# A DFT and MLP kernel: four of eight blocks of the first DFT as seven products, means added by transfers, the MLP begun by token halves

## The chip, the cores and the metric

The kernel runs on one core of one Trainium2 chip. The metric is the time on the device in microseconds. PE is TensorE, DVE VectorE, ACT ScalarE, POOL GpSimd; SP issues most transfers.

## The reference

All is float32: 2048 tokens (S) of 512 features (D), an MLP of 1792 hidden units (F).

```python
xn = layernorm(x)
a = einsum("bsd,ed->bse", xn, dft_hid_re)      # first DFT, along the features
b = einsum("bsd,ed->bse", xn, dft_hid_im)
s = einsum("ts,bse->bte", dft_seq_re, a) - einsum("ts,bse->bte", dft_seq_im, b)
h = gelu(einsum("bsd,df->bsf", layernorm(xn), w1) + b1)
g = silu(einsum("bsf,fd->bsd", h, w2) + b2)
out = x + s * g
```

## The kernel before

Each float32 operand is split into a rounded part `hi` (ACT, L64) and the rest `lo` (DVE, L65), and each product is three matmuls: hi hi, hi lo, lo hi. Big tiles are 128 x 2 x 512 floats from one pool of 39 (`operand`, `guest`); PSUM has eight banks of 128 x 512 in the first stage. The order on each engine is that of the code, written out by hand; engines and queues work in order.

**First DFT.** Row block i is 128 tokens, blocks of four row blocks are "blocks" b of 512 tokens. For each of 16 row blocks and each of the two matrices (m) `dft_mm` (L305) adds 12 matmuls into one bank: four blocks of features, three terms each. `dft_out` (L328) copies the bank out on ACT with the row's factor and leaves the store in a list that is four long (LAG) before SP issues it. Row blocks 0 to 3 are centred and transposed on PE (`first_x`, `first_transpose`); for blocks 1 to 3 the transposed input `xT` is loaded (`xt_load`), and DVE subtracts the row of means (`xt_centre`, L265), after which `xt_make` splits it. A row of means comes from statistics on DVE (L106), is turned on PE (`rows_turn`, L169), copied by ACT, written to DRAM (L173) and read back by SP with a broadcast over the partitions (`row_load`, L177). The factors are computed in small DVE operations (`rstd`). The row R holds the factors of the second layernorm.

**Operands of the MLP.** In the second half of that stage DVE scales the centred `xT` by R (`y_scale`, L409) and makes the sums t1 to t4 of its quarters (`y_sum`, L421); `y_split` splits 11, t1, t2, 21, 22, t3, t4. The first MLP layer then needs seven block products for eight, in chunks j of 7: `h_product` (L518), each 24 matmuls over two halves of tokens (tau). `w1_sums` and `w1_split` make w1's operands of a chunk. After each product `h_after` copies or adds a PSUM tile. The second layer (L684) and the DFT along the sequence (L684, L1002), both by seven products, follow.

Products are numbered as in the code: 1, 6, 7 and 4 accumulate on one PSUM tile ("y"), 5 and 3 on "z", 2 on "x"; the partial sums are taken out between them.

Of the kernel before, what the change touches and what calls it, by code (L numbers as in the profile page):

```python
# [15 lines left out]
P = 128  # L16
# [6 lines left out]
def fnet_mixer_kernel(ctx: ExitStack, tc: tile.TileContext, x, xT, ct, wt, w1, w2, b1, b2, out):  # L23
# [71 lines left out]
    r1 = consts.tile([P, NS], F32, name="r1")  # L95
    nr1 = consts.tile([P, NS], F32, name="nr1")
    r2 = consts.tile([P, NS], F32, name="r2")
    v2 = consts.tile([P, NS], F32, name="v2")
# [11 lines left out]
    def rstd(r, var, i, n):  # L110
        v = small.tile([P, n], F32, tag="v", name="v")
# [3 lines left out]
        ops = [  # L115
            lambda: nc.vector.tensor_scalar(v, var, EPS, None, op0=ALU.add),
            lambda: nc.vector.tensor_scalar(h.bitcast(I32), v.bitcast(I32), 1, None, op0=ALU.logical_shift_right),
            lambda: nc.vector.tensor_scalar(y.bitcast(I32), h.bitcast(I32), -1.0, float(RSQRT_MAGIC), op0=ALU.mult,
                                            op1=ALU.add),
            lambda: nc.vector.tensor_scalar(h, v, -0.5, None, op0=ALU.mult),  # L120
        ]
        for k in range(4):
            dst = r[:, i:i + n] if k == 3 else y
            ops += [
                lambda: nc.vector.tensor_mul(t, y, y),
                lambda: nc.vector.tensor_mul(t, t, h),
                lambda dst=dst: nc.vector.scalar_tensor_tensor(dst, t, 1.5, y, op0=ALU.add, op1=ALU.mult),
            ]
        return ops


    def weave(chain, others):
        n = max(len(chain), len(others))
        at = 0
        for q, o in enumerate(chain):
            o()
            while at * len(chain) < (q + 1) * len(others):
                others[at]()
                at += 1
        for o in others[at:]:  # L140
            o()

    def r1_chain(i, n):
        return rstd(r1, mv1[:, i:i + n, 1], i, n) + [
            lambda: nc.vector.tensor_scalar(nr1[:, i:i + n], r1[:, i:i + n], -1.0, None, op0=ALU.mult)]

    def r2_chain():
        return [lambda: nc.vector.tensor_mul(v2, mv1[:, :, 1], r1),  # L150
                lambda: nc.vector.tensor_mul(v2, v2, r1)] + rstd(r2, v2, 0, NS) + [
                lambda: nc.vector.tensor_mul(r2, r2, r1)]
# [43 lines left out]


# [3 lines left out]
    def x_load(i):  # L201
        if i % 2 == 0:
            x_two[i // 2] = guest(f"x{i}")
        xs[i] = x_two[i // 2][:, i % 2, :]
        nc.sync.dma_start(out=xs[i], in_=x[i * P:(i + 1) * P, :])

    raw_w = []


    def load_w(m, k2):  # L210
        t = room(f"rw{m}{k2}")
        for k in (2 * k2, 2 * k2 + 1):
            (nc.scalar if m == 0 and k % 2 else nc.sync).dma_start(out=t[:, k % 2, :], in_=wt[m, k])
            raw_w.append(t[:, k % 2, :])

# [41 lines left out]
    def xt_load(b):  # L257
        for k2 in range(NK // 2):
            xtr[b, k2] = guest(f"xT{b}_{k2}")
            nc.sync.dma_start(out=xtr[b, k2], in_=xT[b, 2 * k2:2 * k2 + 2].rearrange("k p w -> p k w"))  # L260
# [25 lines left out]
    MEANS = {1: "m1", 2: "m02", 3: "m3"}  # L286

    def m_pack(b):
        rows_pack([mv1[:, block(int(c)), 0] for c in MEANS[b][1:]], MEANS[b])

    def m_turn(b):
        rows_turn(MEANS[b])
        blocks = [int(c) for c in MEANS[b][1:]]
        for c, row in zip(blocks, row_load(MEANS[b], len(blocks))):
            mrow[c] = row
# [27 lines left out]

    def dft_out(i, m):
# [3 lines left out]
        nc.scalar.activation(e, dacc.pop((i, m)), AF.Copy, scale=(nr1 if m else r1)[:, i:i + 1])  # L328
        stores.append(((b_d if m else a_d)[i // 2][i % 2], e))
# [23 lines left out]
    xt_load(1)  # L353

# [8 lines left out]
    m_pack(1)  # L363
    first_x(3)
    dft_mm(1, 1)
    m_turn(1)
    weave(r1_chain(0, 2 * NC), [])
# [5 lines left out]
    for q in range(2 * NC, 3 * NC):  # L373
        x_load(q)
# [3 lines left out]
    def xt_prepare(b, ks):  # L378
        for k in ks:
            xt_centre(b, k)  # L380
        for k in ks:
# [25 lines left out]
    def y_scale(k2, bs):  # L407
        for b in bs:
            nc.vector.tensor_mul(xtr[b, k2], xtr[b, k2], both(rrow[b]))  # L409
            y_raw[(("11", "12"), ("21", "22"))[k2][b // 2], b % 2] = xtr[b, k2]  # L410

    def y_split(name):
        y_op[name] = [split_two(y_raw[name, tau], f"y{name}_{tau}") for tau in range(2)]

    def y_sum(dst, a, b):
        for tau in range(2):
            if dst == "t1":
                y_raw["t1", tau] = guest(f"yt1_{tau}")
            if dst in ("t2", "t3", "t4"):
                y_raw[dst, tau] = y_raw[{"t2": "t1", "t3": "12", "t4": "t2"}[dst], tau]  # L420
            nc.vector.tensor_sub(y_raw[dst, tau], y_raw[a, tau], y_raw[b, tau])  # L421

    for i in range(3, NS):
        b, c = divmod(i, NC)
        chain, bulk = [], []
        if b == 0:
            xt_prepare(1, range(NK // 2))
        elif b + 1 < NB:
            if i == 4:
                xt_load(2)  # L430
            if i == 6:
                xt_prepare(2, (0, 1))
            if i in (8, 9):
                xt_prepare(3, (i - 8,))
        if i == 4:
            for q in range(3 * NC, 4 * NC):
                x_load(q)
            early.close()
            wr = early.enter_context(tc.tile_pool(name="wr", bufs=1, reuse_waits="tile"))
            wp = early.enter_context(tc.tile_pool(name="wp", bufs=4, reuse_waits="tile"))  # L440
            lp = early.enter_context(tc.tile_pool(name="lpm", bufs=2, reuse_waits="tile"))
            w1_load(0)
        if i in (4, 5):
            bb = i - 2
            bulk = [lambda q=q: stats(mv1, xs[q], q) for q in range(bb * NC, (bb + 1) * NC)
                    ] + [lambda: m_pack(bb)]
        if i == 6:
            xt_load(3)
        if i == 7:
            chain = r1_chain(2 * NC, 2 * NC) + r2_chain()  # L450
            xt_load(0)
        if i == 10:
            for k2 in range(2):
                xt_centre(0, k2)
        if i == 11:
            y_scale(0, (0, 1, 2))
        if i == 12:
            y_scale(0, (3,))
            y_split("11")
            y_sum("t1", "12", "11")  # L460
        if i == 13:
            y_split("t1")
            y_scale(1, (2, 3))
        if i == 14:
            y_sum("t2", "22", "t1")
            y_split("t2")
        if i == 15:
            y_sum("t3", "22", "12")
            y_scale(1, (0, 1))
        weave(chain, bulk)  # L470
        if i == 7:
# [586 lines left out]
```

## Time and profile before

| | |
|---|---|
| median of 3 runs | 675.45 us (675.4 to 675.48) |
| span of the profiled execution | 673.0 us |
| first matmul of the first DFT | 6.18 us |
| first matmul of the MLP | 96.39 us |
| transfers | 171.49 MB, mean 255 GB/s |

Each row of a timeline has the start and the duration in us, engine, line, operation, the tile written and those read, their shapes, how many in a row, and in brackets how long the engine stood idle before and what ended that. "PEld" is the load of a stationary operand. A row that ends in "q" after the engine is a transfer being issued. In a row of windows each pair is busy time and number of instructions for PE, PEld, DVE, ACT and POOL, then the granted clock of PE, the busy share of the transfer engines and GB/s. The clock stays at full speed in the stage in question.

### The profile page before, as it was taken

How to read it: one execution, taken by the hardware profiler on the slowest of the kernel's cores; microseconds unless marked ns; L12 is line 12 of the kernel's file. 1: busy time of each engine (PE TensorE's matmuls, PEld its weight loads, DVE VectorE, ACT ScalarE, POOL GpSimd, SP SyncE). 2: the span in 40 equal slices, each digit the busy share in tenths (PEclk: the TensorE clock that was granted, in tenths of full speed). 3: DMA queues.
4: the chain of work that ended last, by engine and by line, in shares of the span. 5: the costliest groups of instructions: out<-in, count | busy, mean ns of one | idle time of the engine just before them, and what ended most of it. 6: DMA issues, size and time to landing. Idle time of an engine off the chain costs nothing.

```text
span 673.0 us, 8182 instructions
## 1 busy us (share of the span) xinstructions
PE 665.8 (99%) x2933; PEld 547.5 (81%) x2933; DVE 538.3 (80%) x595; ACT 346.9 (52%) x366; POOL 47.0 (7%) x80
## 2 busy tenths in 40 slices
PE   8999999999999999999999999999999999999996
PEld 5888888888888888888888888888888888888885
DVE  7877887777778755887988998729978399998995
ACT  4443666445454665565546555446445454646540
POOL 1000000122112100000000100000000001210100
PEclk9999999999999999999999999999999999999999
DMA  8667731899998999588799997406545548996883
GB/s 312 225 222 233 261 131 58 311 331 327 329 337 305 415 376 362 188 281 289 277 371 409 390 321 255 157 32 196 190 154 146 127 123 259 303 257 243 307 259 126
DMA packets 69896, 171.49 MB, mean 255 GB/s; under 512 B 6592, under 2 KB 20960, under 8 KB 69856
## 3 DMA queue, kind: packets, MB, share of 16 engines
q1 hardware_dynamic: 58304, 132.67, 56.4%
q0 software_dynamic: 11200, 37.76, 17.2%
q8 instruction: 23, 0.38, 0.2%
q10 hardware_dynamic: 352, 0.54, 0.2%
q14 instruction: 17, 0.14, 0.1%
HBM read 120.60 MB, written 50.35 MB: 254 GB/s over the span
## 4 chain that ended last, share of the span: by engine, by line
PE 97%; DVE 1%; DMA 1%; issue 0%; ACT 0%; SPq 0%; DVEq 0%
PE pz L684 19%; PE px L684 18%; PE pd L305 12%; PE ma L684 11%; PE hy L518 11%; PE mb L684 8%; PE hz L518 6%; PE pw L684 5%; PE hx L518 3%; PE px L1002 2%; PE pw L1002 2%; DVE W L279 1%; DMA rw<-wt 1%; PE pt L250 0%; DVE zr L1007 0%
## 5 line engine op out<-in xcount | busy, mean ns | idle before, releaser
L790 DVE TENSOR_TENSOR c<-c,c 128x1024 f32<-128x1024 f32 x32 | 39.0, 1218 | 3.2 <-DMA c<-ct 3.2
L65 DVE TENSOR_TENSOR w1l<-w1r,w1h 128x1792 fp32r<-128x1792 f32 x7 | 14.2, 2025 | 24.5 <-ACT w1h L64 24.5
L65 DVE TENSOR_TENSOR R_b1l<-c,R_b1h 128x1024 fp32r<-128x1024 f32 x16 | 19.4, 1221 | 13.9 <-ACT R_b1h L64 10.6
L305 PE MATMUL pd<-W,xt_0h 128*128 128x512 f32 x96 | 29.8, 392 | 0.0
L684 PE MATMUL pw<-R_s1h,L 128*128 128x512 f32 x96 | 29.7, 389 | 0.0
L305 PE MATMUL pd<-W,xt_1h 128*128 128x512 f32 x96 | 29.6, 389 | 0.0
L64 ACT ACTIVATE R_s3h<-c 128x1024 fp32r<-128x1024 f32 x16 | 17.0, 1061 | 23.6 <-DVE c L790 9.5
L64 ACT ACTIVATE R_b2h<-c 128x1024 fp32r<-128x1024 f32 x16 | 16.9, 1059 | 21.5 <-DVE c L795 13.4
L523 ACT ACTIVATE hc<-hc,b_t 128x1024 f32<-128x1024 f32 x14 | 16.1, 1153 | 20.3 <-DVE hc L558 19.7
L65 DVE TENSOR_TENSOR R_s2l<-c,R_s2h 128x1024 fp32r<-128x1024 f32 x16 | 19.5, 1221 | 8.6 <-PE pz L684 8.6
L64 ACT ACTIVATE R_s2h<-c 128x1024 fp32r<-128x1024 f32 x16 | 17.0, 1061 | 16.7 <-PE px L684 9.3
L65 DVE TENSOR_TENSOR R_s3l<-c,R_s3h 128x1024 fp32r<-128x1024 f32 x16 | 19.5, 1219 | 3.9 <-PE pz L684 3.9
L64 ACT ACTIVATE R_s1h<-c 128x1024 fp32r<-128x1024 f32 x16 | 16.4, 1051 | 11.7 <-DVE c L801 11.7
L64 ACT ACTIVATE R_b1h<-c 128x1024 fp32r<-128x1024 f32 x16 | 16.6, 1052 | 11.0 <-PE pz L684 5.5
L64 ACT ACTIVATE R_a1h<-c 128x1024 fp32r<-128x1024 f32 x16 | 16.9, 1054 | 8.9 <-PE pz L684 7.2
L305 PEld LDWEIGHTS pd<-W,xt_1h 128*128 128x128 f32 x96 | 18.0, 188 | 3.8
L684 PEld LDWEIGHTS pw<-R_s1h,L 128*128 128x128 f32 x96 | 18.0, 188 | 3.7
L798 POOL DMA_DIRECT2D c<-ct x8 | 6.9, 868 | 201.5 <-issue 141.6
L305 PEld LDWEIGHTS pd<-W,xt_0h 128*128 128x128 f32 x96 | 17.8, 188 | 4.0
L65 DVE TENSOR_TENSOR R_b2l<-c,R_b2h 128x1024 fp32r<-128x1024 f32 x16 | 19.4, 1218 | 1.5 <-PE px L684 1.5
L65 DVE TENSOR_TENSOR R_a1l<-c,R_a1h 128x1024 fp32r<-128x1024 f32 x16 | 19.5, 1219 | 1.3 <-PE px L684 1.1
L65 DVE TENSOR_TENSOR R_s4l<-c,R_s4h 128x1024 fp32r<-128x1024 f32 x16 | 19.5, 1218 | 0.7 <-PE px L684 0.7
(886 smaller groups left out, 2172.9 us busy)
## 6 DMA issues: line engine op xcount, KB each, us to landing
c<-ct SPq DMA_DIRECT2D x68, 512.0 KB, 5.9
m<-h_d SPq DMA_DIRECT2D x48, 512.0 KB, 6.8
h_d<-ht POOLq DMA_DIRECT2D x21, 512.0 KB, 7.6
s_d<-sa SPq DMA_DIRECT2D x32, 256.0 KB, 4.0
la<-s_d SPq DMA_DIRECT2D x32, 256.0 KB, 5.5
h_d<-hc POOLq DMA_DIRECT2D x13, 512.0 KB, 4.0
x<-x SPq DMA_DIRECT2D x16, 256.0 KB, 5.0
xT<-xT SPq DMA_DIRECT2D x8, 512.0 KB, 6.1
```

What stands on the lines that cost most here:

```text
L64: nc.scalar.activation(hi, src, AF.Copy)
L65: nc.vector.tensor_sub(lo, src, hi.bitcast(F32))
L279: nc.vector.tensor_sub(lo, raw_w[n], hi.bitcast(F32))
L305: nc.tensor.matmul(acc, xt[i, k][px], weights[m * NK + k][pw], start=n == 0, stop=n == len(terms) - 1)
L518: nc.tensor.matmul(acc[:, tau, :], w[:, W1_AT[p], k * P:(k + 1) * P], r[:, k, :], start=p in (1, 5, 2) and i == 0, stop=p in (2, 3, 4) and ...
L523: nc.scalar.activation(dst, src, AF.Gelu_apprx_tanh, bias=b1_t[:, row:row + 1])
L684: nc.tensor.matmul(acc[k][:, tau, :], a, c[:, tau, :], start=first and i == 0, stop=last and i == len(terms) - 1, skip_group_check=True)
L790: nc.vector.tensor_sub(t, t, raw)
L798: nc.gpsimd.dma_start(out=t, in_=ct[1, 1, n], accum_op=ALU.add)
L1002: nc.tensor.matmul(acc[KEY[name]][k][:, tau, :], a[k], c[:, tau, :], start=False, stop=u == us[-1] and i == 2, skip_group_check=True)
```

## The change

Row blocks 0 to 7 (now the token blocks 0 and 2, by `tok`) go through `dft_mm` as before. The other eight (token blocks 1 and 3) are computed behind them as seven block products of 24 matmuls (`q_product`): left operands are the split MLP operands of token half 1 (`y_op[name, 1]`), right ones the split sums of the DFT matrices' quarters, which `a_sums` makes and `a_split` splits. As the MLP operands carry the second layernorm's factor, `q_after` multiplies by a factor `qq` that takes it off: for products 1, 5, 6, 4 a copy on ACT, for 2, 3, 7 a `scalar_tensor_tensor` on DVE that adds a bank to the copy. Product 4 accumulates on the bank that product 7's `q_after` has read.

Only block 1 is still centred by DVE and split as a DFT operand. For the other three the negative means are written over a tile with a broadcast (SP, two loads of 256 KB) and `xT` is added to it by an accumulating transfer on POOL's queue (`centred_load`). Row blocks 12 to 15 get their statistics from two activations with an accumulated sum on ACT (`act_stats`).

The DVE operations that make operands are handed to `q_product` as steps, one behind each block of four. The first chunk of the MLP runs all products but the fourth on token half 1 (ONE), then on half 0 (ZERO); w1 is loaded and split during the seven products, where before it was done in row blocks 4 to 10.

The core of the diff (in the loop, only what stands there now; the lines removed are printed above):

```diff
+    def second_factors():
+        for make, at in ((outer, 0), (inner, HB)):
+            make(vv[:, at:at + NC], mv1[:, HB:HB + NC, 1], 1.0)
+            make(vv[:, at + NC:at + HB], sq, 1.0 / D)
+        rsqrt(rr[:, 2 * HB:], vv, 2 * HB)
+    def last_factors():
+        nc.vector.tensor_mul(qq, vv[:, :HB], rr[:, 2 * HB:3 * HB])
+        nc.vector.tensor_mul(qq, qq, rr[:, 3 * HB:])
+        nc.vector.tensor_scalar(nq, qq, -1.0, None, op0=ALU.mult)
...
+    TB = (0, 2, 1, 3)
+    def tok(i):
+        return TB[i // NC] * NC + i % NC
...
+    NEG = {2: 0, 3: 1, 0: 2}
+    def neg_means(b):
+        nc.vector.tensor_scalar(nm[:, block(NEG[b])], mv1[:, block(b), 0], -1.0, None, op0=ALU.mult)
+    def act_stats(i):
+        t = guest(f"as{i}")
+        c = i % NC
+        nc.scalar.activation(t[:, 0, :], xs[i], AF.Copy, scale=-1.0 / D, accum_out=nm[:, NC + c:NC + c + 1])
+        nc.scalar.activation(t[:, 1, :], xs[i], AF.Square, bias=nm[:, NC + c:NC + c + 1], accum_out=sq[:, c:c + 1])
+    def centred_load(b):
+        row = row_d["n"][0, NEG[b] * W:(NEG[b] + 1) * W].partition_broadcast(P)
+        for k2 in range(NK // 2):
+            t = xtr[b, k2] = guest(f"xT{b}_{k2}")
+            for k in range(2):
+                nc.sync.dma_start(out=t[:, k, :], in_=row)
+            nc.gpsimd.dma_start(out=t, in_=xT[TB[b], 2 * k2:2 * k2 + 2].rearrange("k p w -> p k w"), accum_op=ALU.add)
...
     xt_load(1)
+    for q in range(NC):
+        x_load(3 * NC + q)
...
-    m_turn(1)
-    weave(r1_chain(0, 2 * NC), [])
+    m_turn()
+    first_factors()
...
-    for q in range(2 * NC, 3 * NC):
-        x_load(q)
+    act_stats(3 * NC)
+    act_stats(3 * NC + 1)
+    for q in range(NC):
+        x_load(2 * NC + q)
...
+    def y_scale(k2, b):
+        nc.vector.tensor_mul(xtr[b, k2], xtr[b, k2], both(rrow[b]))
+        y_raw[f"{k2 + 1}{b % 2 + 1}", b // 2] = xtr[b, k2]
+    def y_split(name, tau):
+        y_op[name, tau] = split_two(y_raw[name, tau], f"y{name}_{tau}")
+    def y_sum(dst, tau):
+        place, a, b = {"t1": ("11", "12", "11"), "t2": ("t1", "22", "t1"), "t3": ("12", "22", "12"),
+                       "t4": ("t2", "21", "t2")}[dst]
+        t = y_raw[dst, tau] = y_raw[place, tau]
+        nc.vector.tensor_sub(t, y_raw[a, tau], y_raw[b, tau])
+    a_op = {}
+    def a_sums():
+        a11, a12, a21, a22 = (room_w[m, k2] for m in range(2) for k2 in range(2))
+        nc.vector.tensor_add(a22, a21, a22)
+        nc.vector.tensor_sub(a21, a11, a21)
+        nc.vector.tensor_sub(a11, a22, a11)
+        nc.vector.tensor_sub(a12, a12, a11)
+    def a_split(p):
+        m, k2 = {5: (1, 1), 6: (0, 0), 3: (0, 1), 7: (1, 0)}[p]
+        hi, lo = split_two(room_w[m, k2], f"A{p}")
+        a_op[p] = [(hi[:, k, :], lo[:, k, :]) for k in range(2)]
+    RIGHT = {1: "11", 2: "21", 3: "22", 4: "t4", 5: "t1", 6: "t2", 7: "t3"}
+    qx, q_part = {}, {}
+    def q_place(name, c):
+        if c % 2 == 0:
+            q_part[name, c] = guest(f"q{name}_{c}")
+        return q_part[name, c - c % 2][:, c % 2, :]
+    def q_out(i, m, e):
+        stores.append((dft_at(i, m), e))
+        while len(stores) > LAG:
+            store()
+    def q_after(p, c):
+        i, j = 2 * NC + c, 3 * NC + c
+        f, g = (qq[:, t - HB:t - HB + 1] for t in (i, j))
+        nf, ng = (nq[:, t - HB:t - HB + 1] for t in (i, j))
+        acc = qx[{1: "y", 6: "y", 7: "y", 4: "y", 5: "z", 3: "z", 2: "x"}[p], c]
+        if p in (1, 5, 6, 4):
+            e = q_place(p, c)
+            nc.scalar.activation(e, acc, AF.Copy, scale={1: f, 5: ng, 6: g, 4: nf}[p])
+            if p == 4:
+                q_out(i, 1, e)
+        else:
+            e = q_part[{2: 1, 3: 6, 7: 5}[p], c - c % 2][:, c % 2, :]
+            nc.vector.scalar_tensor_tensor(e, acc, {2: f, 3: g, 7: ng}[p], e, op0=ALU.mult, op1=ALU.add)
+            q_out(*{2: (i, 0), 3: (j, 0), 7: (j, 1)}[p], e)
+    def q_product(p, steps=()):
+        key = {1: "y", 6: "y", 7: "y", 4: "y", 5: "z", 3: "z", 2: "x"}[p]
+        yh, yl = y_op[RIGHT[p], 1]
+        for c in range(NC):
+            if p in (1, 5, 2):
+                qx[key, c] = bank(f"q{key}{c}")
+            cols = slice(c * P, (c + 1) * P)
+            terms = [(a[:, k, cols], w) for k in range(2)
+                     for a, w in ((yh, a_op[p][k][0]), (yh, a_op[p][k][1]), (yl, a_op[p][k][0]))]
+            for n, (a, w) in enumerate(terms):
+                nc.tensor.matmul(qx[key, c], a, w, start=p in (1, 5, 2) and n == 0,
+                                 stop=p in (2, 3, 4) and n == len(terms) - 1, skip_group_check=True)
+            q_after(p, c)
+            if c < len(steps):
+                steps[c]()
+    for i in range(3, HB):
+        if i == 3:
+            xt_prepare(1)
+            act_stats(3 * NC + 2)
+            act_stats(3 * NC + 3)
+            for q in range(NC):
+                stats(mv1, xs[2 * NC + q], 2 * NC + q)
+            neg_means(2)
+            neg_means(0)
         if i == 4:
+            second_factors()
+        if i == 5:
+            a_sums()
+            last_factors()
         if i == 6:
+            y_scale(0, 2)
+            y_split("11", 1)
         if i == 7:
+            y_scale(1, 2)
+            y_split("21", 1)
+            a_split(5)
         dft_mm(i, 0)
         dft_out(i - 1, 1)
+        if i == 5:
+            row_st["R"] = rr[:, HB:3 * HB]
             rows_turn("R")
+            rrow = [None] * 2 + row_load("R", 2, 2)
         dft_mm(i, 1)
         dft_out(i, 0)
+        if i == 4:
+            row_st["n"] = nm
+            rows_turn("n")
+            centred_load(2)
+            centred_load(3)
+    dft_out(HB - 1, 1)
+    for p, (m, k2) in {1: (0, 0), 2: (0, 1), 4: (1, 1)}.items():
+        a_op[p] = [weights[m * NK + 2 * k2 + k] for k in range(2)]
+    y_scale(0, 3)
+    y_sum("t1", 1)
+    y_split("t1", 1)
+    q_product(1, [lambda: y_scale(1, 3), lambda: y_sum("t2", 1)])
+    rrow[0:2] = row_load("R", 2)
+    centred_load(0)
+    q_product(2, [lambda: y_split("t2", 1), lambda: a_split(6)])
+    q_product(5, [lambda: y_split("22", 1), lambda: a_split(3), lambda: y_sum("t3", 1), lambda: y_split("t3", 1)])
+    q_product(6, [lambda: a_split(7), lambda: y_sum("t4", 1), lambda: y_split("t4", 1)])
+    early.close()
+    wr = early.enter_context(tc.tile_pool(name="wr", bufs=1, reuse_waits="tile"))
+    wp = early.enter_context(tc.tile_pool(name="wp", bufs=4, reuse_waits="tile"))
+    lp = early.enter_context(tc.tile_pool(name="lpm", bufs=2, reuse_waits="tile"))
+    w1_load(0)
+    q_product(3, [lambda: y_scale(0, 0), lambda: y_scale(0, 1), lambda: y_split("11", 0)])
+    def w1_make(j):
+        w1_sums(j)
+        w1_split(j)
+        w1_load(j + 1)
+    q_product(7, [lambda: y_sum("t1", 0), lambda: w1_make(0), lambda: y_split("t1", 0)])
+    q_product(4, [lambda: y_scale(1, 1), lambda: y_sum("t2", 0), lambda: y_split("t2", 0), lambda: y_scale(1, 0)])
...
+    ONE, ZERO = slice(1, 2), slice(0, 1)
+    h_seq = [(0, p, s) for s in (ONE, ZERO) for p in (1, 5, 6, 2, 3, 7)]
+    for j in range(1, NJ):
+        h_seq += [(j, 1, TAUS), (j, 5, TAUS), (j - 1, 4, TAUS), (j, 6, TAUS), (j, 2, TAUS), (j, 3, TAUS), (j, 7, TAUS)]
+    y_late = {(1, ONE): lambda: y_split("21", 0),
+              (5, ONE): lambda: y_split("22", 0),
+              (6, ONE): lambda: y_sum("t3", 0),
+              (2, ONE): lambda: y_split("t3", 0),
+              (3, ONE): lambda: w1_make(1),
+              (3, ZERO): lambda: (y_sum("t4", 0), y_split("t4", 0))}
```

`h_product` and `h_after` take the halves as a slice, with the same matmuls.

More of the change, by code (lines that the diff above doesn't have):

```diff
@@ L122, in rstd @@
-        for k in range(4):
[L123 to L141, printed above, removed]
@@ new lines, in outer, with first_factors @@
+    def outer(dst, var, scale):
+        nc.vector.tensor_scalar(dst, var, scale * (1.0 + EPS), EPS * EPS, op0=ALU.mult, op1=ALU.add)
+    def first_factors():
+        v = small.tile([P, 2 * HB], F32, tag="v", name="v")
+        inner(v[:, :HB], mv1[:, :HB, 1], 1.0)
+        outer(v[:, HB:], mv1[:, :HB, 1], 1.0)
+        rsqrt(rr[:, :2 * HB], v, 2 * HB)
+        nc.vector.tensor_scalar(nr1, rr[:, :HB], -1.0, None, op0=ALU.mult)
+    def second_factors():
[3 more added lines that the diff above has]
+        rsqrt(rr[:, 2 * HB:], vv, 2 * HB)
@@ L327, in dft_out @@
         e = e_two[i][:, m, :]
-        nc.scalar.activation(e, dacc.pop((i, m)), AF.Copy, scale=(nr1 if m else r1)[:, i:i + 1])
-        stores.append(((b_d if m else a_d)[i // 2][i % 2], e))
+        nc.scalar.activation(e, dacc.pop((i, m)), AF.Copy, scale=(nr1 if m else rr)[:, i:i + 1])
+        stores.append((dft_at(i, m), e))
         while len(stores) > LAG:
```

207 lines of the change are left out of this document (67 added, 140 removed).

## The prediction

> **What bounds the kernel now.** I read the busy times, the chain of waits, the waits of PE, then the timeline of the first 125 us, where the change lies, and the transfers last.
>
> ```profile
> span 673.0 us, 8182 instructions
> ...
> PE 665.8 (99%) x2933; PEld 547.5 (81%) x2933; DVE 538.3 (80%) x595; ACT 346.9 (52%) x366; POOL 47.0 (7%) x80
> ...
> PE 97%; DVE 1%; DMA 1%; issue 0%; ACT 0%; SPq 0%; DVEq 0%
> ...
> PE idle_ps L189 <- DVE warm L217: 1.2, 1, 1.2
> PE pd L320 <- ACT xt L64: 0.4, 1, 0.4
> PE pt L250 <- DVE xc L240: 0.3, 1, 0.3
> ...
> 96.39 0.39 PE L518 MATMUL hy<-y_0h,w1h 128*128 128x512 f32 x1
> ...
> 99.11 0.39 PE L518 MATMUL hz<-yt_0h,w1h 128*128 128x512 f32 x1
> ```
>
> PE is the bound, and it waits 1.9 us in all, before 7 us. So every matmul taken away is worth its full slot, and every new wait of PE costs its full length. Twelve matmuls lie between the two starts: 2.72 / 12 = 0.227 us each. The MLP starts at 96.39, right behind the first DFT: that is the mark against which I place the new stage.
>
> **What is removed.** Blocks of 24 matmuls: 16 row blocks before (384), now 8 (192) and 7 products of 4 x 6 (168). 24 fewer x 0.227 = -5.44 us. One transpose of rows fewer (m1, n, R for four) is about -0.25. If nothing else changed, the time would fall to 669.8.
>
> **New ACT work ahead of block 4.** The four `act_stats` activations of row blocks 12 and 13 stand on ACT between the copies of row block 1 and that of 2, so ahead of the rounding `xt_0h`, for which PE waits.
>
> ```profile
> 2.03 0.20 ACT L218 ACTIVATE warm<-warm 128x1 f32<-128x1 f32 x1
> ...
> 6.29 2.71 ACT L278 ACTIVATE W<-rw 128x512 fp32r<-128x512 f32 x5
> ...
> 25.93 0.72 ACT L328 ACTIVATE e<-pd,r 128x512 f32<-128x512 f32 x1
> ...
> 26.80 1.06 ACT L64 ACTIVATE xt_0h<-xT 128x1024 fp32r<-128x1024 f32 x1 [0.15 <-DVE xT L265]
> ...
> 29.04 1.22 DVE L65 TENSOR_TENSOR xt_1l<-xT,xt_1h 128x1024 fp32r<-128x1024 f32 x1
> ...
> 30.43 0.41 PEld L305 LDWEIGHTS pd<-W,xt_0h 128*128 128x128 f32 x2
> ...
> 31.79 0.41 PEld L305 LDWEIGHTS pd<-W,xt_1l 128*128 128x128 f32 x2
> ...
> 18.00:20.00 2.00, 2.00 (x11) 1.55 (x10) 1.86 (x6) 0.27 (x1) 0.00 (x0) 1.00 0.00 0
> ```
>
> No row shows an activation with an accumulated sum. From below: five 128x512 copies in 2.71, a pace of 0.52, so 2.1 for four. From above: the longest copy of that shape, 0.72, and a small operation of 0.20, so 3.7. I take the middle, 2.9. `xt_1l` ends at 30.26 and is loaded at 31.79, a margin of 1.53, and ACT has 0.15 of slack before `xt_0h`. `first_factors` is one small operation longer and twice as wide, 0.3. So PE waits 2.9 + 0.3 - 1.53 - 0.15 = 1.5 us (0.7 to 2.3) as row block 4 starts. The moved loads of x cost nothing: the transfers stand still from 18 to 20 us, which covers the extra 1 MB; without that cover the m1 row would be late by up to some 3 us.
>
> **The way of the means (n).** They are turned behind row block 4: 30.43 + 1.5 + 24 x 0.227 = 37.4.
>
> ```profile
> 38.81 0.27 PE L169 MATMUL rpm<-ident,rsm 128*8 128x128 f32 x1
> ...
> 40.64 0.32 SPq L177 DMA_DIRECT2D rowm<-rdm  x1
> ...
> rowR<-rdR SPq DMA_DIRECT2D x2, 512.0 KB, 5.3
> z_d<-z POOLq DMA_DIRECT2D x2, 512.0 KB, 3.3
> ...
> rowm<-rdm SPq DMA_DIRECT2D x2, 256.0 KB, 3.4
> ...
> L798 POOL DMA_DIRECT2D c<-ct x8: 850/860/912, 515.6 to 595.3; - x8
> ...
> DMA to landing us min/median/max: 5.3/7.5/10.1
> ...
> L937 POOL DMA_DIRECT2D p<-xT x6: 1197/1202/1282, 581.2 to 634.9; - x6
> ...
> DMA to landing us min/median/max: 9.2/10.5/12.7
> ...
> L937 POOL DMA_DIRECT2D p<-xT x2: 1200/1241/1282, 633.8 to 634.9; - x2
> ...
> DMA to landing us min/median/max: 9.3/10.3/11.3
> ```
>
> From transpose to row load are 1.83 us, so SP issues at 39.2. `xT2_0` needs two loads of 256 KB, the first two of eight: between 3.4 (one of 256 KB) and 5.3 (one of 512 KB), I take 4.5, so 43.7. Then POOL issues the accumulating transfer. Its nearest rows land after 5.3 to 10.1 and 9.2 to 12.7; p<-xT has the same 2 KB runs but met full queues, c<-ct has longer ones. I take 8.5, between the medians, so **L = 52.2** (49.0 to 56.4). Two issued 1.1 apart (633.8, 634.9) landed 3.1 apart, so the other three follow by some 3 us each, ahead of their use.
>
> The Trainium skill, "DMA: Bandwidth & Descriptors", section "Anatomy of one DMA — SWDGE (gpsimd) path", fits such a transfer as 2.0 us plus its bytes at 436 GB/s. By that 512 KB would be an estimate of 3.2 us, where the accumulating rows here have 5.3 at the least; with it the sum would be 676.1 in place of 681.4.
>
> **DVE through the seven products.** From L on DVE has one row of work in the order of the code.
>
> ```profile
> 16.92 0.69 DVE L106 BATCH_NORM_STATS2 st<-x 128x6 f32<-128x512 f32 x1
> ...
> 17.74 0.66 DVE L106 BATCH_NORM_STATS2 st<-x 128x6 f32<-128x512 f32 x1
> ...
> 20.07 0.16 DVE L116 TENSOR_SCALAR v<-mv 128x8 f32<-128x8 f32 x1
> ...
> 20.95 0.17 DVE L126 TENSOR_TENSOR tv<-tv,hv 128x8 f32<-128x8 f32 x1
> ...
> 22.96 0.17 DVE L127 SCALAR_TENSOR_TENSOR r<-tv,y 128x8 f32<-128x8 f32 x1
> ...
> 24.94 0.69 DVE L65 TENSOR_TENSOR xt<-pt,xt 128x512 fp32r<-128x512 f32 x1 [1.61 <-ACT xt L64]
> ...
> 56.72 1.23 DVE L265 TENSOR_TENSOR xT<-xT,rowm 128x1024 f32<-128x1024 f32 x1 [0.38 <-DMA rowm<-rdm]
> ...
> 57.98 1.06 ACT L64 ACTIVATE xt_0h<-xT 128x1024 fp32r<-128x1024 f32 x1 [7.09 <-DVE xT L265]
> ...
> 59.08 1.22 DVE L65 TENSOR_TENSOR xt_0l<-xT,xt_0h 128x1024 fp32r<-128x1024 f32 x1 [1.13 <-ACT xt_0h L64]
> ...
> 65.98 0.42 DVE L393 TENSOR_TENSOR w1r<-w1r 128x256 f32<-128x256 f32 x1
> ...
> 69.30 2.02 DVE L65 TENSOR_TENSOR w1l<-w1r,w1h 128x1792 fp32r<-128x1792 f32 x1 [1.77 <-ACT w1h L64]
> 71.24 4.63 DVE L409 TENSOR_TENSOR xT<-xT,rowR 128x1024 f32<-128x1024 f32 x4
> ```
>
> Four 128x1024 operations take 4.63, a pace of (4.63 - 1.22) / 3 = 1.14. Where DVE makes a tile and then needs ACT's rounding of it, it idles: 56.72 + 1.14 to 59.08 is 1.2. `w1_make` is 65.98 to 71.24, 5.3. The new `scalar_tensor_tensor` on a PSUM bank is not shown; at 128x8 that operation and the plain one both take 0.17, so I price it as the plain 128x512 one on PSUM, at most 0.69, pipelined 0.64 (a gain is excluded, all twelve are new).
>
> Up to the correction of product 7's third block DVE does: scales, sums and splits of 11, 21, A5, t1, t2, A6, 22, A3, t3, A7, t4, of token half 0's 11, and its t1 sum, in all 23 x 1.14 = 26.2; 11 corrections x 0.64 = 7.0; `w1_make` 5.3; waits for ACT's rounding behind 11, 21, t1, t3, t4 (1.2 each) and in part t2 and A7 (0.6, 0.5) 7.1. Together L + 45.6. PE's last product, 4, adds onto the same bank, so its third block can't start before. It then takes 6 x 0.227 = 1.36 (47.0); the fourth waits for one more split and correction (47.4); the stage ends at **L + 48.7 = 100.9**.
>
> PE alone would be sooner. DVE ends block 1's split at 30.26 + 0.3 + 2.9 - 0.15 = 33.3, does four statistics (17.74 - 16.92 = 0.82 each, 36.6) and the 21 small operations of `neg_means` and `second_factors` at (22.96 - 20.07) / 15 = 0.19, 40.6; PE asks for R half a row block behind n, at 37.4 + 0.25 + 2.72 = 40.4. I put that wait at 0.3. Row blocks 5 to 7 end at 37.4 + 16.3 + 0.3 and two transposes of 0.25, 54.5, and 168 matmuls on PE would be done at 92.6. DVE's lateness costs 8.3, in parts: 0.8 before product 1 (it needs 11's rest, `lo`, at its third matmul: scale, rounding and rest end at L + 3.6, less 0.45, so it starts at L + 3.1), some where product 5 takes product 2's banks, the rest in product 4. DVE can't begin sooner: from `last_factors` on it stands at the scale that waits for L. ACT stands there too, with five banks behind it; eight suffice.
>
> **The seam.** Sixteen half products take PE as long as eight whole ones, so the halves themselves cost nothing, the split being covered by half 1's products. But DVE comes late with the w1 operands of chunk 1 (`w1_make(1)`, now at half 1's product 3, was done at 71 before), by about 0.4, and with the add of half 0's product 7, for which (0, 4) waits, by about 1.1. Together 1.5 (0 to 2.5). Thereafter DVE's 20% of idle time pays the rest.
>
> **Sum.** 100.9 - 96.4 = +4.5, with 1.5 for the seam +6.0. By terms: -5.44 - 0.25 + 1.5 + 0.3 + 8.3 + 1.5 = +5.9. Against the profiled span, 673.0 + 6.0 = 679.0; the median shown, 675.45, lies 2.45 above that span, so **681.4**. The bounds of L and the seam give 676.7 to 686.
>
> **Rivals.** *PE keeps the bound* (faster side): DVE's row fits, and only the ACT wait and R's are left: 675.45 - 5.69 + 1.8 = 671.6, or 669.8 without them. For it: DVE has about 20% idle over the span, and the sum of its work, 38.5 without waits up to the point above, is close to PE's 38.1. It holds if DVE starts these steps some 8 us before I think, so L near 44; against it: L would have to come at the very landing of the rows, and even a DVE abreast of PE at product 7 has `w1_make`, 5.3, between corrections that PE wants 1.36 apart.
>
> *Quick accumulation*: the transfer lands as a plain store on POOL's queue, 3.3 (the z_d row). L = 47.0, stage end 95.7, with the seam's 1.5 it is 676.2; with a seam of nothing 674.7. For it: apart from the rows the queues are light then. Against it: all 14 accumulating rows. The skill's formula above speaks for this rival.
>
> *Crowded queues*: eight row loads, R's row, stores and four accumulations meet; the first lands 12.7 after its issue, at 56.4, the stage ends at 105.1: 685.6. For it: p<-xT under load; against: the mean traffic there is two row blocks' stores.
>
> **Chances.** Forecast 0.62; PE bound 0.16; quick accumulation 0.12; crowded 0.10. About 0.2% (1.35 us) is what a measurement can tell from no change. Faster: 0.16 and a little of the quick case, 0.18; same 0.08, from that case; slower 0.74. The range 674.0 to 686.0 leaves out most of the PE-bound case and the upper end of crowding, some 2 in 10.
>
> **What would show it.** Right: PE waits for DVE in product 4's third and fourth block, of several us, and in product 5; DVE idle until `xT2_0` lands near 52; MLP start near 101; a PE wait near 30 us that ends on ACT's or DVE's block 1 operands. Wrong: DVE abreast of PE at product 7, the MLP starting near 91, or an accumulating transfer under 5 us.

## The result and the profile after

The changed kernel takes **706.45 us** (median of 4 runs, 705.58 to 706.76), against 675.42 for the kernel before on the same chip: 1.0459 times as long, 95% interval 1.0444 to 1.0474. The direction was right; the size, 681.4 with a range up to 686, was far too small. Busy times, the chain of waits and PE's own waits of the profile after:

```profile
span 704.1 us, 8163 instructions
...
PE 676.0 (96%) x2908; PEld 548.1 (78%) x2908; DVE 538.9 (77%) x585; ACT 353.5 (50%) x387; POOL 54.4 (8%) x86
...
PE 84%; DVE 7%; DMA 4%; ACT 3%; issue 1%; SPq 0%; ACTq 0%; DVEq 0%
...
PE qy L503 <- ACT y_1h L64: 8.7, 1, 8.7
PE hy L601 <- DVE hc L654: 5.3, 1, 5.3
PE qy L503 <- DVE q L490: 3.9, 1, 3.9
PE hy L601 <- ACT hc L614: 1.9, 1, 1.9
```

PE's share of the chain falls from 97% to 84%. Four waits make up 19.8 us: one ahead of the first of the seven products (`y_1h`), one in product 4 (`q`, the third block behind product 7's correction, as forecast), and two in the MLP's first group. The waits alone do not explain the 31.1 us by which the span grew: 24 matmuls fewer should have paid 5.4 of them. So PE is slower, too. The windows show where:

```profile
55.00:59.40 4.40, 0.00 (x0) 0.00 (x0) 0.00 (x0) 0.00 (x0) 0.83 (x1) 1.00 1.08 281
59.50:62.00 2.50, 0.00 (x0) 0.00 (x0) 0.90 (x1) 0.00 (x0) 0.00 (x0) 0.50 1.10 257
...
66.00:69.60 3.60, 3.60 (x10) 2.73 (x10) 2.67 (x3) 3.58 (x5) 0.00 (x0) 0.50 1.06 347
69.80:72.00 2.20, 2.20 (x11) 1.76 (x11) 1.85 (x2) 0.28 (x1) 0.00 (x0) 1.00 1.05 344
...
107.30:110.60 3.30, 3.30 (x8) 2.62 (x9) 3.27 (x4) 0.35 (x1) 0.00 (x0) 0.50 0.92 243
...
114.07:117.48 3.41, 1.52 (x7) 0.96 (x6) 2.08 (x3) 2.55 (x4) 0.00 (x0) 1.00 0.71 274
...
117.50:120.80 3.30, 3.30 (x9) 2.53 (x9) 2.31 (x2) 1.96 (x3) 0.00 (x0) 0.50 0.00 0
...
131.30:134.50 3.20, 3.20 (x9) 2.51 (x8) 0.00 (x0) 0.60 (x1) 0.00 (x0) 0.50 0.77 264
```

The number behind the five busy times is the granted clock. PE stands idle from 55, the clock falls to 0.50 at about 59.5, and is back at 1.00 at 69.8, though PE works again from 63.47; at 0.50 it does 10 matmuls in 3.6 us, at 1.00 11 in 2.2. The same happens behind the wait in product 4 (107.3) and twice in the MLP's first group (117.5 and 131.3), there also behind the wait of only 1.9 us that ends at 116.53. The prediction has no word of this.

The spells of half clock run from 59.45 to 69.69, 107.24 to 110.65, 117.48 to 120.89 and 127.72 to 134.55, and all eight of these times lie whole multiples of 3.41 us apart. So the clock changes here only at the edges of a grid. That is why it stays low for 6.2 us of work behind the first wait: in the stretch from 62.86 to 66.28 PE is busy for 2.77 of 3.42 us, and the first stretch that it works through is the next, 66.28 to 69.69. The Trainium skill, "TensorE: Matmul & The Clock Gate", section "Part 1: The HAM clock gate (the "warmup" mystery)", states half clock after an idle window of some 3.4 us and full clock after as long a busy one, with windows that run free of the kernel. The trace agrees on the windows and on the way back; but before the fall at 117.48 the window was not idle: PE was busy for 1.52 of its 3.41 us.

The timeline to the point where DVE begins its row of work (L of the prediction, the start of the first scaling by R), SP and POOL first, then DVE, and the times from issue to landing of the transfers' lines in the same order (`rdR`'s write, the row loads `xT<-rdn`, four accumulating transfers, the later two, R's row):

```profile
39.97 6.22 SPq L315 DMA_DIRECT2D xT<-rdn  x8
...
48.88 0.95 SPq L174 DMA_DIRECT2D rowR<-rdR  x1
...
45.91 1.24 POOL L316 DMA_DIRECT2D xT<-xT  x1 [43.20 <-DMA xT<-rdn]
...
61.10 1.23 DVE L436 TENSOR_TENSOR xT<-xT,rowR 128x1024 f32<-128x1024 f32 x1 [15.14 <-DMA rowR<-rdR]
...
DMA to landing us min/median/max: 6.9/6.9/6.9
...
DMA to landing us min/median/max: 3.9/6.8/9.0
...
DMA to landing us min/median/max: 12.6/14.8/16.2
...
DMA to landing us min/median/max: 6.2/6.7/7.2
...
DMA to landing us min/median/max: 8.5/10.3/12.1
```

Three things came later than forecast: the rows under the first tile (45.9 for 43.7), the accumulating transfer (12.6 for 8.5, so 58.5), and R's row, for which no time had been set at all: issued at 48.88 and 12.1 in coming, it ends DVE's wait at 61.0. From there DVE's row is as forecast. The last rows of it, and PE's start on the MLP:

```profile
106.48 0.74 DVE L490 SCALAR_TENSOR_TENSOR q<-qy,nq,q 128x512 f32<-128x512 f32 x1
...
108.28 0.74 DVE L490 SCALAR_TENSOR_TENSOR q<-qy,nq,q 128x512 f32<-128x512 f32 x1
...
111.68 0.40 PE L601 MATMUL hy<-y_1h,w1h 128*128 128x512 f32 x1
```

Product 7's third correction ends at 107.22, L + 46.1 (forecast L + 45.6), the fourth at L + 47.9 (L + 47.4); the MLP starts at L + 50.6 (L + 48.7), the rest being product 4 at half clock.

The MLP's first group, DVE and PE:

```profile
122.68 0.42 DVE L421 TENSOR_TENSOR w1r<-w1r 128x256 f32<-128x256 f32 x1
...
125.99 2.03 DVE L65 TENSOR_TENSOR w1l<-w1r,w1h 128x1792 fp32r<-128x1792 f32 x1 [1.76 <-ACT w1h L64]
...
128.53 0.68 DVE L654 TENSOR_TENSOR hc<-hc,hy 128x512 f32<-128x512 f32 x1
...
129.26 0.80 PE L601 MATMUL hy<-y_0h,w1h 128*128 128x512 f32 x1 [5.34 <-DVE hc L654]
```

PE's row is half 0's product 1. Its operands are long there; it waits for half 1's last addition (L654), which reads the other bank of the same tile `hy`, and which stands on DVE behind `w1_make(1)`. After the group nothing is lost: from the second MLP layer's first matmul to the last matmul it is 440.5 us, and 440.4 before.

But from the MLP's first matmul to the second layer's it is 146.1 us (111.68 to 257.76) against 130.6 (96.39 to 226.96), 15.5 more, and the two waits there, 5.3 and 1.9, are half of that. Matmuls of the first layer alone, in the same window at full clock, before and after, with the pairs of PE and PEld alone:

```profile
160.00:220.00 60.00, 60.00 (x267) 49.67 (x266) 1.00 0.91 329
...
160.00:220.00 60.00, 60.00 (x259) 48.35 (x258) 1.00 0.88 323
```

267 matmuls in 60 us before, 259 after, without a wait: 3.1% slower over all of the layer's 588 matmuls, 588 x 0.227 x 0.031 = 4.1 us. The remaining 15.5 - 7.2 - 4.1 = 4.2 are the half clock: matmuls start 0.43 apart there in place of 0.23, in 3.4 us of work up to 120.89 and 5.3 us up to 134.55, and 8.7 x (1 - 0.233 / 0.427) = 4.0.

### The profile page after: what moved, and what is told of

The parts are those of the page before. It is cut to its first block, busy times and chain, and to the rows that moved or that the text cites. A ratio compares the mean times of both kernels' runs of the same rounds, so it can differ in the third digit from the quotient of the medians.

```text
span 704.1 us, 8163 instructions
## 1 busy us (share of the span) xinstructions
PE 676.0 (96%) x2908; PEld 548.1 (78%) x2908; DVE 538.9 (77%) x585; ACT 353.5 (50%) x387; POOL 54.4 (8%) x86
## 4 chain that ended last, share of the span: by engine, by line
PE 84%; DVE 7%; DMA 4%; ACT 3%; issue 1%; SPq 0%; ACTq 0%; DVEq 0%
PE pz L776 19%; PE px L776 17%; PE ma L776 11%; PE hy L601 11%; PE mb L776 8%; PE hz L601 5%; PE pw L776 5%; PE hx L601 3%; PE pd L326 2%; DMA rowR<-rdR 2%; PE px L1094 2%; PE pw L1094 2%; DMA b_d<-e 1%; DVE xT L447 1%; DVE xT L436 1%
## 5 line engine op out<-in xcount | busy, mean ns | idle before, releaser
L882 DVE TENSOR_TENSOR c<-c,c 128x1024 f32<-128x1024 f32 x32 | 39.0, 1219 | 4.2 <-DMA c<-ct 4.2
L606 ACT ACTIVATE hc<-hc,b_t 128x1024 f32<-128x1024 f32 (+1 forms) x16 | 16.7, 1045 | 22.1 <-DVE hc L644 19.9
L64 ACT ACTIVATE R_b1h<-c 128x1024 fp32r<-128x1024 f32 x16 | 16.6, 1052 | 12.7 <-DMA c<-ct 6.7
L436 DVE TENSOR_TENSOR xT<-xT,rowR 128x1024 f32<-128x1024 f32 x8 | 9.7, 1218 | 15.1 <-DMA rowR<-rdR 15.1
L887 DVE TENSOR_TENSOR c<-c,c 128x1024 f32<-128x1024 f32 x16 | 19.6, 1224 | 0.4
L64 ACT ACTIVATE R_s4h<-c 128x1024 fp32r<-128x1024 f32 x16 | 16.8, 1051 | 5.2 <-PE pz L776 4.8
L64 ACT ACTIVATE w2h<-w 128x1024 fp32r<-128x1024 f32 (+1 forms) x14 | 13.2, 946 | 11.9 <-DVE w L712 3.9
```

The lines of the kernel that those rows point to most:

```text
L64: nc.scalar.activation(hi, src, AF.Copy)
L606: nc.scalar.activation(dst, src, AF.Gelu_apprx_tanh, bias=b1_t[:, row:row + 1])
L882: nc.vector.tensor_sub(t, t, raw)
L887: nc.vector.tensor_add(raw, raw, t)
```

## The experiments

All edits are to the changed kernel (706.45 us). L is the start of the first scaling by R on DVE, "MLP" its first matmul, "layer" the time from there to the second layer's first matmul, all of the profiled run.

| run | median, us | L | MLP | layer |
|---|---|---|---|---|
| before | 675.42 | - | 96.39 | 130.6 |
| after | 706.45 | 61.10 | 111.68 | 146.1 |
| e1_align | 702.23 | 60.93 | 111.39 | 142.6 |
| e2_seam | 698.95 | 61.45 | 112.89 | 138.4 |
| e10_halves | 703.23 | 61.19 | 111.71 | 144.3 |
| e5_warm | 703.23 | 60.37 | 112.38 | 142.5 |
| e3_centre | 699.52 | 49.66 | 104.82 | 146.4 |
| e6_rfirst | 707.89 | 57.06 | 115.90 | 144.5 |
| e7_reorder | 699.39 | 60.38 | 105.38 | 145.3 |
| e8_all | 680.65 | 48.57 | 95.17 | 137.5 |
| e9_best | 679.18 | 48.71 | 95.33 | 135.5 |
| e11_best2 | 681.81 | 49.12 | 95.70 | 136.4 |

**e1_align: why the layer's matmuls are slower.** The new constants (`rr`, `vv`, `qq` and others) moved the pools behind them: by the tile sizes, as I reckon them (no trace records an address), w1's split operands began at a multiple of 128 bytes in each partition before, and begin 64 bytes off one after. The edit takes 64 bytes out of a tile that is only a spacer.

```diff
-    consts.tile([P, 3 * W // 32], F32, name="spare")
+    consts.tile([P, 2 * W // 32], F32, name="spare")
```

> Only the spare tile is 64 bytes shorter, so that the tiles behind it (w1's split operands among them) start where they did before the change, at a multiple of 128 bytes instead of 64 beyond one. Theory: the 588 matmuls of the first MLP layer went from 0.2267 to 0.2333 us each because of that address; they go back, 588 x 0.0067 = 3.9 us, 702.5 us. Rival: the slower pace comes from the transfers or from the clock after the stalls; the pace stays 0.2333 and the time 706.4.

702.23, ratio to before 1.0393 (1.0378 to 1.0409): 4.2 us sooner, as expected. The same window of its profile:

```profile
160.00:220.00 60.00, 60.00 (x267) 49.67 (x266) 1.00 0.89 326
```

267 again. So 64 bytes ahead of the pools cost 3% of the pace. Of what these matmuls read and write only the stationary operand, w1's split tiles, lies behind the spacer, so I put the cost to its address. Tiles of the other engines moved with it, and that these play no part is not shown.

**e2_seam: the seam's wait.** `w1_make(1)` moves behind the addition for which PE waits.

```diff
-              (3, ONE): lambda: w1_make(1),
+              (1, ZERO): lambda: w1_make(1),
```

> The making of w1's second chunk is moved on DVE from ahead of half 1's last two additions to behind them. Theory: half 0's first product waits for half 1's last addition on the same PSUM tile, though they use different halves of it; that addition comes 4.5 us sooner, PE's wait of 5.3 falls under 1, and with it the half clock of 127.7 to 134.5 (2.7 us more): 706.4 - 7.2 = 699.2. Rival 1: w1's second chunk is then late for chunk 1 by as much: 704 or more. Rival 2: PE waits there for an operand of half 0: 706.4.

698.95, ratio 1.0345 (1.0328 to 1.0363), as expected; 7.5 us from moving one step. Its waits of PE:

```profile
PE hy L601 <- ACT hc L614: 1.6, 2, 1.0
PE hy L601 <- DVE hc L654: 1.6, 1, 1.6
```

The wait fell by 3.7 only; the layer by 7.7. The rest, 4.0, is half clock: the granted clock from 120 to 140 us is 1.00 here, 0.81 after, and neither of the layer's two spells is left. Not all of this is the edit's doing. The spell from 117.48 followed the wait for ACT, which lies ahead of the step that was moved; here that wait is 1.0 at the longest and falls otherwise in the clock's grid. In return product 4's spell lasts 6.8 us for 3.4, and the MLP starts 1.2 later.

**e10_halves: is it the shared tile?** The two halves' accumulators of "y" and "x" change places in half 0, so that half 0's y no longer lies beside half 1's.

```diff
+    def hx_at(j, key, s):
+        if j == 0 and s == ZERO:
+            key = {"y": "x", "x": "y", "z": "z"}[key]
+        return hx[j, key][:, s, :]
```

> The changed kernel with one difference: in the MLP's first group the accumulators of the two token halves no longer share a tile (half 0's y accumulator lies beside half 1's x accumulator, and the other way round), so that no instruction on one half is ordered behind the other half's last addition. The arithmetic and its order are as before. Theory (the 5.3 us wait of half 0's first product is the shared tile alone, and the half clock behind it follows from that idleness): the wait goes, and with it some 2 us of half clock: 698 to 700 us, against 706.45. Rival (half 0 would wait for DVE anyway, for the operands that are still being split): the wait only moves to a later product of half 0, 704 us or more.

703.23, ratio 1.0401 (1.0375 to 1.0427), four runs from 700.82 to 705.00: between the two. The profile is of a run of 704.46.

```profile
PE hz L605 <- DVE hu L660: 3.3, 1, 3.3
PE hy L605 <- ACT hc L623: 1.9, 1, 1.9
```

The wait on `hy` is gone without any step of DVE being moved, so the shared tile made it. But the "z" accumulators I had left on one tile, and half 0's product 5 now waits 3.3 us on it, for half 1's other addition, again behind `w1_make(1)`. The operands of half 0 end no wait here either. My estimate overlooked the second tile.

**e5_warm: what the half clock costs.** Matmuls on zeros, into banks that are free, fill PE's idle stretches; the outputs do not depend on them.

```diff
+    def fill(ps, n):
+        for q in range(n):
+            nc.tensor.matmul(ps, idle[:, :P], idle, start=True, stop=True)
...
+    fill(bank("fill"), 40)
     q_product(1, ...)
```

and 18 ahead of product 4's third block, 24 ahead of half 0's product 1.

> Idle matmuls on zeros fill PE's three long waits: 40 ahead of product 1, 18 ahead of the third block of product 4, 24 ahead of half 0's first product. Theory: the granted clock falls to a half where PE has been idle for some 4 us, and that costs time of its own only where PE is the last: 1.4 in product 4, 1.5 in half 1's products and 2.7 in half 0's, while product 1's slowness is hidden behind DVE: clock 1.00 throughout, 706.4 - 5.6 = 700.8. Rival 1: all of the half clock counts, 8.7 us: 697.7. Rival 2: the clock falls for another reason than idleness: it stays at 0.98, and the time at 706.4 or above.

703.23, ratio 1.041 (1.0394 to 1.0425): 3.2 us sooner, between the 5.6 expected and the nothing of rival 2. The window from 60 to 80 us:

```profile
60.00:80.00 20.00, 17.21 (x74) 12.25 (x73) 15.73 (x15) 12.97 (x17) 2.37 (x2) 1.00 0.99 276
```

With PE kept busy the clock stays at 1.00 (0.76 after, in the same window), so idleness made it fall. Product 4's last matmul starts 1.85 sooner (109.60 for 111.45), but the MLP does not (112.38). Its first product waits 2.4 us for ACT's copy of a bank of product 4 (`q`), a wait that the changed kernel does not have; probably the two banks of the filling shift which bank the MLP takes first, but that was not tried. A spell of half clock stands there, from 111.95 to 115.37. The gain is all in the MLP's first layer (146.1 to 142.5), and part of that is the wait of 1.9 for ACT, which is gone here. So the 3.2 is a net figure, and the price of the half clock is better read from the spells above.

**e3_centre: the centring transfers.** Blocks 2 and 3 are loaded plainly and early, and DVE adds the row of negative means; block 0 keeps its transfers.

```diff
+    xt_load(2)
+    xt_load(3)
     dft_mm(2, 1)
...
-            centred_load(2)
-            centred_load(3)
+            mrow[2], mrow[3] = row_load("n", 2)
```

with `xt_centre` ahead of each `y_scale` of these blocks.

> Blocks 2 and 3 (token blocks 1 and 3) are loaded plainly, early, and centred by DVE with one row load of 512 KB, as before the change; only block 0 keeps the accumulating transfers. Theory: the row of DVE work starts when the R row is there, near 47.7 in place of 61.1; PE doesn't wait before product 1 and keeps its clock there; two subtractions more lie in the row, so the MLP starts near 99 in place of 111.7: 693.5 us. Rival 1: PE, not DVE, sets the products' end, which is then at 92.7: 687. Rival 2: the two megabytes loaded early push the statistics and rows back by what they save: above 702.

699.52, ratio 1.0352 (1.0337 to 1.0367): the size was wrong.

```profile
49.66 1.23 DVE L438 TENSOR_TENSOR xT<-xT,rowR 128x1024 f32<-128x1024 f32 x1 [2.10 <-DMA rowR<-rdR]
...
PE hy L605 <- DVE hc L658: 6.9, 1, 6.9
PE qy L505 <- DVE q L492: 4.2, 1, 4.2
PE qz L505 <- DVE q L492: 3.3, 1, 3.3
```

L comes 11.4 us sooner and product 1 starts without a wait. But three centrings of 1.2 us now lie behind L, and PE waits for DVE in products 5 and 4: the MLP starts 6.9 sooner, and that is the gain. DVE's row bounds these products from its start on, at 49.7 as at 61.1.

**e6_rfirst: which transfer ends DVE's wait.** R's row load goes ahead of block 3's transfers on SP.

```diff
             centred_load(2)
-            centred_load(3)
...
             rrow = [None] * 2 + row_load("R", 2, 2)
+            centred_load(3)
```

> On SP's queue the load of the R row is put ahead of the last four of the eight loads of mean rows. Theory: R's row is only the last of two late things; the first accumulating transfer landed at 58.5 and R's row at 61.0, so DVE's row of work starts at 56 to 58.5, and the time falls by 2.6 to 5: 701.5 to 704. Rival: the queue of rows ahead of R is the cause alone; R lands near 50, DVE starts there, and the time falls by some 11: 695.

707.89, ratio 1.0479 (1.0464 to 1.0495): neither.

```profile
42.32 0.38 SPq L363 DMA_DIRECT2D b_d<-e  x1
48.91 0.32 SPq L174 DMA_DIRECT2D rowR<-rdR  x1
...
57.06 1.23 DVE L436 TENSOR_TENSOR xT<-xT,rowR 128x1024 f32<-128x1024 f32 x1 [10.59 <-DMA rowR<-rdR]
...
PE qz L503 <- DVE q L490: 5.9, 1, 5.9
PE qy L503 <- ACT y_1h L64: 4.1, 1, 4.1
```

SP stands still from 42.7 to 48.9 for the small write of R, so the load is issued no sooner than before. It lands in 8.1 for 12.1, L is 4 us sooner, and product 1's wait falls from 8.7 to 4.1; then block 3's transfers, which stood behind R, cost 5.9 in product 5. R's way, write and load, took 6.9 + 12.1 us after, 6.8 + 8.1 here, and 3.1 + 4.3 in e3_centre, where only a single row load stood with it: it is the traffic of the centring that delays it.

**e7_reorder: DVE's waits for ACT.** The steps of the seven products are put in another order, with another step between the making of a tile and its split, and w1's `lo` behind product 7; half 0's t2 split goes to the MLP's first product.

```diff
-    y_scale(0, 3)
-    y_sum("t1", 1)
-    y_split("t1", 1)
-    q_product(1, [lambda: y_scale(1, 3), lambda: y_sum("t2", 1)])
+    y_scale(0, 3)
+    y_sum("t1", 1)
+    y_scale(1, 3)
+    y_split("t1", 1)
+    q_product(1, [lambda: y_sum("t2", 1), lambda: a_split(6)])
...
-    q_product(7, [lambda: y_sum("t1", 0), lambda: w1_make(0), lambda: y_split("t1", 0)])
+    q_product(7, [lambda: w1_high(0), lambda: y_split("t1", 0)])
```

> The order of DVE's steps alone: behind each making of a tile stands another step ahead of its split, and the rest of w1's first chunk is made behind product 7's corrections; one split moves to the MLP's first product. Theory: DVE is the bound of the products; it loses some 5.5 us of waiting for ACT's roundings and 3.8 us of w1 ahead of product 7's last corrections, so that PE sets their end again: 105 in place of 111.7, and the half clock at 107 to 110 goes: about 697.5 us. Rival 1: the length of DVE's row doesn't matter, since the late start and PE's half clock set the end: 705 or more. Rival 2: what is taken from the products comes back in the MLP's first chunk, where DVE is late already: 702.

699.39, ratio 1.0354 (1.0338 to 1.0369), between the 697.5 of the theory and the 702 of rival 2.

```profile
PE qy L503 <- ACT y_1h L64: 8.3, 1, 8.3
PE hy L613 <- DVE hc L666: 6.9, 1, 6.9
...
PE qy L503 <- DVE q L490: 0.8, 1, 0.8
```

Product 4's wait of 3.9 falls to 0.8, and the MLP starts at L + 45.0 in place of L + 50.6. A part came back at the seam (6.9 for 5.3).

**e8_all: the edits together.** e1_align, e3_centre's loads and e7_reorder's order, with `w1_make(1)` at half 0's product 5, that product first in half 0, and other places for DVE's splits in the first group.

> Four things together: blocks 2 and 3 centred by DVE on early plain loads, the order of DVE's steps with waits filled, w1's second chunk behind half 1's additions with half 0 begun by product 5, and the 64 bytes. Theory: with the row of DVE work begun near 49.7 and no waits in it, its last correction is due near 91.4 and PE's products end at 93.3, with nothing of the half clock left; the MLP starts at 93.5 to 94.5 and loses about 1 in its first chunk: 673 to 675 us, a little under the kernel before. Rival 1: DVE is still some us late at product 7: 677 to 681. Rival 2: buffers or queues that were hidden so far come up: above 681.

680.65, ratio 1.0074 (1.0058 to 1.0091): the case of rival 1. 25.8 us of the 31 come back; the MLP starts 1.2 sooner than before the change, and the layer takes 6.9 longer.

```profile
PE hz L618 <- DVE hu L667: 3.0, 1, 3.0
PE hy L618 <- ACT hc L631: 1.5, 2, 0.8
```

Two waits in the MLP's first group are left. The first is the tile "z" again.

**e9_best and e11_best2: is there a version that wins?** e9_best adds to e8_all the accumulators of e10_halves (now with the order 1, 5, 2, 6, 3, 7 in both halves) and `act_stats` behind `xt_prepare(1)`; w1's second chunk is made in two parts, at half 1's product 6 and at half 0's product 1.

> The combination measured at 680.65 us (plain loads of blocks 2 and 3 centred by DVE, DVE's steps reordered, the 64 bytes taken out of the constants), and three more edits: the accumulators of the two halves apart as in the run beside it, the sixth product of each half one place later so that ScalarE's copy has two products of time, and the statistics on ScalarE behind the operands of block 4. Theory: the remaining waits of that run go (3.0 at half 0's fifth product, 1.5 for the copies, 1.2 at block 4, some 1.7 of half clock behind the 3.0), less up to 1 us of a new wait for the second group's weights: 673.5 to 675.5 us, no slower than the kernel before. Rival (DVE's row of work is full up to the second group, so a wait that is removed only comes back there): 677 us or more.

679.18, ratio 1.0053 (1.004 to 1.0066). The waits that were taken away did go, and others came:

```profile
PE hy L622 <- ACT hu L640: 3.0, 1, 3.0
PE qz L503 <- DVE q L490: 1.7, 1, 1.7
```

e11_best2 takes these two on, with two centrings in DVE's wait for R and half 1's product 6 ahead of its 2 again:

```diff
             xt_centre(2, 0)
+            xt_centre(2, 1)
+            xt_centre(3, 0)
             y_scale(0, 2)
-            xt_centre(2, 1)
```

> The version of 679.18 us with its remaining waits taken one by one: two centrings moved into the 3.3 us that DVE waits for R's row (against the 1.7 us before half product 5 of the DFT and 0.8 us behind it), and half 1's sixth product back ahead of its second, so that ScalarE's copy stands before the activation that held it (against the 3.0 us wait and the spell of half clock, some 1.7 us, behind it; up to 0.8 us may come back at the sixth product). Theory: 672 to 674 us, faster than the kernel before. Rival (the waits move on, since DVE's row of work is full): 677 us or more.

681.81, ratio 1.0082 (1.0068 to 1.0097), no gain: the rival.

```profile
PE qz L503 <- DVE q L490: 2.0, 1, 2.0
PE hy L622 <- DVE hc L681: 1.9, 1, 1.9
...
51.48 1.23 DVE L65 TENSOR_TENSOR y_1l<-xT,y_1h 128x1024 fp32r<-128x1024 f32 x1 [1.13 <-ACT y_1h L64]
...
60.00:70.00 10.00, 7.74 (x33) 5.47 (x31) 9.93 (x11) 7.87 (x11) 1.45 (x2) 1.00 1.07 296
```

The centrings that were moved had stood between the scaling of a tile and its split; without them DVE waits 1.13 for ACT's rounding there, and from 60 to 70 us DVE is busy 9.93 of 10. It has no room, and each wait taken away returns at the next product. No version here is as quick as the kernel before, though the last three lie within 1% of it.

## Why the prediction failed

**Right.** Slower, and by this mechanism: PE off the bound, DVE from L on as one row of work. Its length was 46.1 to product 7's third correction, forecast 45.6, and the place of the wait, product 4's third block, was named. `act_stats` cost 2.96 on ACT (26.81 to 29.77), forecast 2.9. PE lost 1.2 us behind it, forecast 1.5: the first eight matmuls of row block 4 took 2.97 us (31.44 to 34.41), and 1.81 before. The block also started 0.8 later than before (31.44 for 30.66), but 0.6 of that was there at `dft_mm`'s first matmul (13.83 for 13.19). The corrections took 0.74 each, 0.66 where two follow each other, forecast 0.64. The rivals "PE keeps the bound" and "quick accumulation" fell with L. But the longest wait, 8.7 us, stands ahead of product 1, for which the prediction had 0.8; product 4's was 3.9. By the prediction's own terms its upper bound is 686.6, not 686; that changes nothing here.

**The step that failed first: L = 52.2.** It was 61.1, 8.9 later. 2.2 of that lie ahead of the accumulating transfer (0.8 as the row loads were issued at 39.97 for 39.2, 1.4 in the loads, which took 3.9 to 9.0 us each among eight, not 4.5), 4.1 the accumulating transfer (12.6, not 8.5), and 2.5 R's row, which the prediction left out of the race. The rival "crowded queues" had the 12.7, but ended on the transfer. e6_rfirst shows that R's row ends the wait, and e3_centre that the crowd is the centring's own: without these transfers L is 49.7. The row that would have warned was in view: loads of 256 KB took 3.4 alone, and the plan put eight of them ahead of R's row on SP's queue, with four transfers of 512 KB on POOL's at the same time.

**The term that was missing: PE's clock.** A PE that waits 8.7 us is not only idle, it is slow for some us after. In product 4 this is about 1.4 us of the 1.9 by which the MLP started later than L + 48.7; in the MLP's first group 4.2 by difference, 4.0 by its two spells. The step "every new wait of PE costs its full length" was too low.

**The term that was mis-sized: the seam, 1.5.** Measured 15.5. The waits are 7.2 of it. 5.3 came because the prediction followed the data (half 0's operands) and not the tile: the order between instructions is kept for whole tiles here, and half 0's first product came behind half 1's last addition (e10_halves). The other 1.9 is half 1's product 6, which waits for ACT to copy product 1's bank; ACT's copy (115.89) stands behind a rounding that itself waits 1.85 us for DVE. That halves "cost nothing" was the wrong sentence. It also had "sixteen half products for eight whole"; there are twelve halves for six. The half clock is 4.2, the address, below, 4.1.

**The term that nobody could read off the diff's operations: 4.1 us of address.** 64 bytes in a pool of constants slowed a layer's matmuls by 3% (e1_align). The shift was readable from the tile sizes in the diff, but no row of before shows the effect.

By terms: 8.9 + 1.9 + (15.5 - 1.5) = 24.8 of the 25.1 us between the forecast span, 679.0, and the measured, 704.1.

**Still open.** How little work in a window of 3.41 us halves the clock is not settled: it fell behind 1.52 us (after, 114.07 to 117.48) and stayed at 1.00 behind 1.67 (e11_best2, 109.30 to 112.70). Whether another way for R (another queue, an earlier turn) would free DVE was not tried. Nor were w1's tiles moved alone. That DVE's full row is what keeps the rearranged versions behind the kernel before was shown by two attempts that failed, not by a version with less work on DVE.

## What to carry to other kernels

Taking work off the bounding engine pays only if the operands that replace it are ready: add up the other engine's row from the last transfer it needs, and put every transfer of that moment on one list, the small rows among them, before choosing which ends last. A stall of PE can cost more than itself, as the clock may halve behind it: in these runs it did behind every wait of 2.4 us or more, and behind some of about 2 us. And when two halves of a tile are to be worked on apart, give them tiles of their own. After any change in the constants compare the pace of untouched matmuls with the pace before.

## What the runs showed of the hardware

- The granted clock fell to 0.50 at 59.45, 4.6 us after PE's last matmul of the row blocks ended, and was 1.00 again at 69.69, 6.2 us after PE went back to work; with PE kept busy it stayed at 1.00 there (e5_warm). Its changes in the changed kernel lie multiples of 3.41 us apart. A wait of 1.9 us was followed by half clock there and by none in e7_reorder and e11_best2.
- Constants that shifted w1's stationary tiles took the matmuls' pace from 267 to 259 in 60 us; 64 bytes less ahead of these tiles brought it back (e1_align).
- Accumulating transfers of 512 KB landed 12.6 to 16.2 us after issue beside eight row loads, 6.2 to 7.2 in the later pair. A write of 8 KB took 6.9 us in that crowd, 3.1 without it (e3_centre).
- An activation with an accumulated sum is followed by a read of the accumulator of 0.18 to 0.23 us:

```profile
28.83 0.19 ACT L306 ACTIVATION_READ_ACCUMULATOR as<-x 128x1 f32 x1
```
